# Left-over keys of P, left-overs of q and k, and whole q, turned as 64-row halves among P's halves

## The chip, the cores and the metric

The kernel runs on one core of a Trainium2 chip. The metric is the device time of one launch in microseconds, as the median of several runs; for each kernel one further execution is profiled. Engines are PE (TensorE, matmul, with PEld for its weight loads), DVE (VectorE), ACT (ScalarE), POOL (GpSimd) and SP (SyncE, which issues the DMAs here).

## The reference

Attention with a bias from the distance of positions, for 4 batches, 8 heads, 576 positions and 64 values per head, and then a layer x @ w_in, h * cos(h), @ w_out on the 2304 rows of its result.

```python
scores = scale * np.matmul(q, k.transpose(0, 1, 3, 2))      # q, k, v: 4 x 8 x 576 x 64
scores = scores + bias.transpose(2, 0, 1)[None, :, :, :]    # bias: a small MLP of log distances
attn = np.exp(scores - np.max(scores, axis=-1, keepdims=True))
attn = attn / (np.sum(attn, axis=-1, keepdims=True) + 1e-09)
x = np.matmul(attn, v)                                      # then as 2304 x 512
h = x @ w_in                                                # 512 x 2048
out = (h * np.cos(h)) @ w_out                               # 2048 x 512
```

All is float32.

## The kernel before

There are three stages: the bias table (to about 58 us), attention (to about 325 us) and the layer behind it. The change touches attention.

**Units and slots.** A unit is a pair of heads and one batch; there are 16, counted from 0. A unit has five jobs, in the order of query tiles 0, 1, 4, 2, 3. Tiles 0 to 3 hold 128 queries for each of the two heads; tile 4 holds the last 64 queries of both. The loop at the end of the attention code calls `slot(i)` for 80 jobs, five slots (j = 0 to 4) per unit, and five more calls stand among the first steps of the next stage. The order of work on each engine is the order of the program: nothing is moved by a scheduler, and each engine takes its instructions in turn.

**What a slot does**, in program order: `qk` makes the scores of this slot's job (L394, tile `s`), and DVE adds the bias and takes the extremum (L407). ACT takes the exponentials of the job before (L427). PE turns the normalised P of the job three slots back: `ptrans` flips it in halves of 64 rows (L456), row tile 0 and row tile 1 in turn, into the two PSUM tiles m0 and m1, eight pairs of flips for tiles 0 to 3 and five for tile 4. Where P has left-over keys 512 to 575 of both heads (tiles 0 to 3), `ptrans_left` turns them as one whole 128x128 block (L469) into the bank `t`, of which there is one. Then come the turns for the next unit (`turn`, L188): in slot 0 k, four whole blocks into bank `t`; in slot 1 "x", the 64 left-over rows of k and of q, one whole block beside the left-over of P in bank `t`; in slot 2 q, four whole blocks into `spare`, a buffer of the two that `s` has. Then PE multiplies earlier turned P with v (`pv`, L518). ACT copies m0 out of PSUM (`keep_main`, L476), then the turned k, x or q (`keep_turned`, L195 to L203), then, where a half of the unit is finished, the result (`keep_x`). DVE takes the row sums and their reciprocals (L439, L442), copies m1 and then the left-over (L479, tiles PT and PX). POOL splits k and q in two parts (L174, L178) and normalises P (L449). Between these, DVE, ACT and POOL widen weights for the next stage (L93 to L111); the weights' loads (L81, L86) are issued in slot 2 of odd units, behind DVE's last read of the buffer (L107).

**Loads.** All are issued by SP, in program order at the end of a slot, by `LOAD_PLAN`: q of the unit after the next in slot 0, k of three units on in slot 2 (two issues for rows 0 to 511 of the heads, L157, and two for the left-over rows of k and q, L160), v of the next unit in slot 4. Slot 1 of unit 0 also loads v of unit 0 and k of unit 2. Units 3, 7 and 11 load the bias of the next pair of heads (L218, L231), two or three issues a slot.

Of the kernel before, what the change touches and what calls it, by code (L numbers as in the profile page):

```python
# [9 lines left out]
F32 = mybir.dt.float32  # L10
# [3 lines left out]
AF = mybir.ActivationFunctionType  # L14
# [14 lines left out]
def kernel(  # L29
# [11 lines left out]
    nc = tc.nc  # L41
    B, H, S, D = q.shape
# [22 lines left out]
    ident = const.tile([128, 128], F32, name="ident")  # L65
# [47 lines left out]
    with tc.manual_schedule():  # L113
# [8 lines left out]
        ld = opened(front, "ld", 2, "right")  # L122
        lk = opened(front, "lk", 2, "right")
# [14 lines left out]

        nat = {}

        def load(u, x):
# [12 lines left out]
            m = 5 if x == "k" else 4  # L154
            t = (lk if x == "k" else ld).tile([128, m, 2, D], F32, tag=x, name=f"n{x}")
            for h in range(2):
                nc.sync.dma_start(out=t[:, 0:4, h], in_=pair_[h, 0:512].rearrange("(p r) d -> p r d", r=4))  # L157
            if x == "k":
# [4 lines left out]
            nat[u, x] = t  # L163

        def split(u, x, step=None):
            n = turned[x]
# [18 lines left out]
        def turn(u, x, ps):  # L185
            n = nat[u, "k" if x == "x" else x].rearrange("p r h d -> p r (h d)")
            for i, c in enumerate((4,) if x == "x" else range(4)):
                nc.tensor.transpose(ps[:, 128 * i : 128 * i + 128], n[:, c], ident)  # L188
            return ps

        def keep_turned(x, ps):
# [10 lines left out]
            o = turned[x][:, 64:576] if x == "k" else turned[x][:, 0:512]  # L202
            nc.scalar.activation(  # L203
                out=o.rearrange("p (x c) -> p x c", c=4),
                in_=ps.rearrange("p (c x) -> p x c", c=4),
                func=AF.Copy,
                scale=-0.125 if x == "q" else 1.0,
            )
# [46 lines left out]
        for x in "kq":  # L255
            load(0, x)
# [14 lines left out]
        pm = bank()  # L271
# [62 lines left out]
        tiles = [0, 1, 4, 2, 3]  # L334
# [35 lines left out]
        ps_s = opened(front, "ps_s", 2, "right", PSUM)  # L370
# [14 lines left out]
        def qk(u, j):  # L385
            t = tiles[j]
            heads = range(2 if t < 4 else 1)
            s = [ps_s.tile([128, 2, 512], F32, tag="s", name="s") for h in heads]
            for hf in range(2):
                for n, (a, b) in enumerate(((0, 0), (0, 1), (1, 0))):  # L390
                    for h in heads:
                        r = slice(64 * h, 64 * h + 64) if t < 4 else slice(0, 128)
                        o = HALF * hf + (64 if h == 0 else 0)
                        nc.tensor.matmul(  # L394
                            s[h][:, hf, 0:HALF],
                            qTs[u % 2][r, a, 128 * t : 128 * t + 128] if t < 4 else qTs[u % 2][:, a, 512:640],
                            kN[u][r, b, o : o + HALF],
                            start=(n == 0),
                            stop=(n == 2),
                            tile_position=(r.start, 0),  # L400
                        )
            hp = units[u][0]
            P[u, j] = pp.tile([128, 1152], F32, tag="p", name="P")
            for h in heads:
                neg = P[u, j][:, 576 * h : 576 * h + 576]
                m = sv.tile([128, 2], F32, tag=f"m{h}", name="m")
                nc.vector.tensor_tensor_reduce(  # L407
                    neg.rearrange("p (a x) -> p a x", a=2),
                    s[h][:, :, 0:HALF],
                    bias[hp, t, h].rearrange("p (a x) -> p a x", a=2),  # L410
                    1.0,
                    3.0e38,
                    ALU.add,
                    ALU.min,
                    m[:, 0:1],
                )
                cur[u, j, h] = (neg, m)
            if t == 4:
                return ps_s.tile([128, 2, 512], F32, tag="s", name="spare")[:, 0]

        P, dn, rc = {}, {}, {}

# [30 lines left out]

        def flip(out, i, r):
            p = slice(64 * r, 64 * r + 64)
            nc.tensor.transpose(out, i[p], ident[p, p], tile_position=(64 * r, 0))  # L456

        def ptrans(u, j):
            ps = [ps_m.tile([128, 512], F32, tag=f"m{r}", name="pm") for r in range(2)]
            cuts = [(256 * h + 64 * c, 640 * h + 128 * c) for h in heads_of((u, j)) for c in range(4)]  # L460
            if tiles[j] == 4:
                cuts.append((256, 512))
            for o, i in cuts:
                for r in range(2):
                    flip(ps[r][:, o : o + 64], P[u, j][:, i : i + 128], r)
            return ps

        def ptrans_left(u, j, ps):
            nc.tensor.transpose(ps, P[u, j][:, 512:640], ident)  # L469

        def where(j):
            t = tiles[j]
# [67 lines left out]
        ]  # L540
        T_EARLY = [(1, "k"), (1, "x"), (1, "q"), None, None]
        PV_EARLY = [[(-1, 0, (0, 1))], [(-1, 0, (2, 3))], [(-1, 0, (4,))], [(-1, 1, (0, 1, 2))], [(-1, 1, (3, 4))]]
        LOAD_PLAN = [[(2, "q")], [], [(3, "k")], [], [(1, "v")]]
        W_PLAN = [("abs", -1), (0, 0), (0.5, 2), (1, 5), (2, 7), ("load", 7), (3, 8), (4, 11)]
        get = lambda i: jobs[i] if 0 <= i < len(jobs) else None

        def slot(i):
            u, j = divmod(i, 5)
            now, last, prev = get(i), get(i - 1), get(i - 3)
            if now:  # L550
                spare = qk(u, j)
            if last:
                for h in heads_of(last):
                    softmax_exp(*last, h)
            if prev:
                if prev[1] in (0, 2):
                    alloc_half(prev[0], prev[1] // 2)
                pm = ptrans(*prev)
            left = prev and tiles[prev[1]] < 4
            tu, tx = T_EARLY[j] or (0, None)  # L560
            tx = tx if now and u + tu < NU else None
            t = bank() if left or tx in ("x", "k") else None
            if left:
                pl = t[:, 0:128]
                ptrans_left(*prev, pl)
            if tx:
                pt = turn(u + tu, tx, {"x": t and t[:, 128:256], "k": t, "q": spare}[tx])
            for du, hf, chunks in PV_EARLY[j]:
                if 0 <= u + du < NU:
                    pv(u + du, hf, chunks)  # L570
            if prev:
                keep_main(*prev, 0, pm[0])
            if tx:
                keep_turned(tx, pt)
            for du, hf, chunks in PV_EARLY[j]:
                if 0 <= u + du < NU and 4 in chunks:
# [17 lines left out]
            if now:  # L594
                if i == 1:
                    load(0, "v")
                    load(2, "k")
                for du, x in LOAD_PLAN[j]:
                    if u + du < NU:
                        load(u + du, x)  # L600
# [243 lines left out]
```

## Time and profile before

| | us |
|---|---|
| median of 3 runs | 727.86 (727.65 to 728.61) |
| the profiled execution | 730.44 |
| its span on the core | 728.60 |
| busy: PE, DVE, ACT, POOL | 712.5, 606.6, 443.9, 405.4 |

The span is the time from the first to the last instruction of the program in the profiled execution; the times of the rows count from its start. A row of a timeline has the start and the length of a run of equal instructions; matmuls are pipelined and their ends are modelled, so that one block's cost is read from its start to the start of the next.

### The profile page before, as it was taken

The numbers are of one execution on the slowest core, as the hardware profiler recorded it, in microseconds if no ns is written. First come the engines' busy times: TensorE is split into PE (matmuls) and PEld (weight loads), VectorE is DVE, ScalarE is ACT, GpSimd is POOL, SyncE is SP. The second block draws the span as 40 slices with busy tenths as digits, with TensorE's granted clock in tenths as the row PEclk, the third lists the DMA queues.
The fourth block names the chain that finished last, engine by engine and source line by source line (L and its number), as shares of the span: only waits on it lengthen the run. The fifth ranks groups of instructions, "written<-read, shape, count | busy, mean of one in ns | idle before, by whom it ended". The sixth has DMA issues, their size and how long they took to land.

```text
span 728.6 us, 15710 instructions
## 1 busy us (share of the span) xinstructions
PE 712.5 (98%) x5786; PEld 571.8 (78%) x5786; DVE 606.6 (83%) x1307; ACT 443.9 (61%) x947; POOL 405.4 (56%) x486
## 2 busy tenths in 40 slices
PE   6997999999999999999999999999999999999997
PEld 3575667766667667669989989988989989989986
DVE  8997788989889888856788789898999999966665
ACT  6897688787778878754565555445454454443342
POOL 0204678888877788874456373564554463663300
PEclk9999899999999999999999999999999999999999
DMA  6787328335432820201011010101011010011113
GB/s 202 239 303 210 91 66 229 78 82 141 135 94 64 232 47 18 76 1 30 30 50 38 32 57 29 59 30 58 30 35 53 29 59 30 0 43 45 45 43 88
DMA packets 84398, 58.65 MB, mean 80 GB/s; under 512 B 62304, under 2 KB 70624, under 8 KB 84320
## 3 DMA queue, kind: packets, MB, share of 16 engines
q1 hardware_dynamic: 84320, 57.63, 27.2%
q8 instruction: 46, 0.75, 0.4%
q14 instruction: 32, 0.26, 0.1%
HBM read 42.00 MB, written 15.61 MB: 79 GB/s over the span
## 4 chain that ended last, share of the span: by engine, by line
PE 95%; DVE 2%; POOL 1%; issue 1%; DMA 0%; ACT 0%; SPq 0%; DVEq 0%
PE ph L644 28%; PE po L699 28%; PE pv L518 13%; PE s L394 11%; PE pa L309 6%; PE pm L456 5%; PE pt L469 2%; PE pt L188 2%; DVE ht L293 1%; PE spare L188 1%; DMA lt<-in_ltab_dram 0%; POOL P L449 0%; DVE P L407 0%; DVE acc L722 0%; POOL kN L178 0%
## 5 line engine op out<-in xcount | busy, mean ns | idle before, releaser
L449 POOL TENSOR_SCALAR P<-P,rc 128x576 f32<-128x576 f32 x144 | 115.0, 812 | 75.7 <-ACT P L427 31.1
L407 DVE CUSTOM_DVE_ANT_0 P<-s,bt 128x576 f32<-128x576 f32 x144 | 103.8, 754 | 29.1 <-PE s L394 19.7
L648 ACT ACTIVATE a<-ph,quarter 128x384 int32<-128x384 f32 x96 | 55.8, 581 | 102.3 <-PE ph L644 101.0
L503 POOL TENSOR_TENSOR xs<-xT,xs 128x384 fp32r<-128x384 f32 x96 | 107.7, 1122 | 8.0
L427 ACT ACTIVATE P<-P,m 128x576 f32<-128x576 f32 x144 | 110.6, 771 | 2.1 <-DVE m L407 1.7
L644 PE MATMUL ph<-xs,wpre 128*128 128x384 f32 x576 | 109.4, 338 | 0.0
L654 DVE SCALAR_TENSOR_TENSOR r<-a,ph 128x384 f32<-128x384 int32 x96 | 52.8, 550 | 67.4 <-ACT a L648 67.2
L644 PE MATMUL ph<-xs,w 128*128 128x384 f32 x576 | 108.3, 337 | 0.0
L644 PEld LDWEIGHTS ph<-xs,wpre 128*128 128x128 f32 x576 | 101.8, 188 | 5.7 <-DVE a L663 0.9
L644 PEld LDWEIGHTS ph<-xs,w 128*128 128x128 f32 x576 | 101.5, 188 | 4.7 <-DVE a L663 0.6
L659 ACT ACTIVATE r<-r,hpi 128x384 f32<-128x384 f32 x96 | 59.3, 617 | 73.5 <-DVE r L655 73.3
L394 PEld LDWEIGHTS s<-kN,qT 64*128 64x128 f32 (+1 forms) x864 | 70.5, 188 | 40.8 <-issue 8.8
L394 PE MATMUL s<-kN,qT 64*128 64x288 f32 (+1 forms) x864 | 93.4, 315 | 4.0 <-DVE m L407 1.8
L502 POOL TENSOR_SCALAR xs<-xT 128x384 fp32r<-128x384 f32 x96 | 62.9, 656 | 39.9 <-PE ph L644 39.9
L518 PE MATMUL pv<-PT,vN 128*64 128x320 f32 (+1 forms) x512 | 76.9, 422 | 0.1
L673 DVE TENSOR_TENSOR gl<-a,gh 128x384 fp32r<-128x384 f32 x96 | 74.3, 774 | 2.2 <-ACT gh L667 2.2
L699 PE MATMUL po<-wpre,gh 128*128 128x512 f32 x288 | 75.3, 397 | 0.0
L699 PE MATMUL po<-w,gh 128*128 128x512 f32 x288 | 75.2, 395 | 0.0
L111 POOL TENSOR_TENSOR w<-wb,w 128x512 fp32r<-128x512 f32 x16 | 20.8, 1298 | 89.2 <-ACT w L109 89.2
L655 DVE SCALAR_TENSOR_TENSOR r<-a,r 128x384 f32<-128x384 int32 x96 | 60.6, 632 | 3.3
L667 ACT ACTIVATE gh<-a 128x384 fp32r<-128x384 f32 x96 | 49.8, 518 | 21.6 <-DVE a L663 21.6
L476 ACT ACTIVATE PT<-pm 128x512 f32<-128x512 f32 (+1 forms) x80 | 44.1, 551 | 30.8 <-PE pm L456 29.5
(83 smaller groups left out, 1220.1 us busy)
## 6 DMA issues: line engine op xcount, KB each, us to landing
sc<-rt SPq DMA_DIRECT2D x36, 295.5 KB, 3.3
raw<-in_moe_w_in_dram SPq DMA_DIRECT2D x16, 512.0 KB, 3.7
raw<-in_moe_w_out_dram SPq DMA_DIRECT2D x16, 512.0 KB, 3.6
bt<-sc SPq DMA_DIRECT2D x16, 288.0 KB, 4.0
nk<-in_k_dram SPq DMA_DIRECT2D x32, 128.0 KB, 3.1
nq<-in_q_dram SPq DMA_DIRECT2D x32, 128.0 KB, 2.9
bt<-sc SPq DMA_DIRECT2D x16, 256.0 KB, 4.0
vN<-in_v_dram SPq DMA_DIRECT2D x32, 128.0 KB, 2.6
```

The costliest lines, as they stand in the source:

```text
L394: nc.tensor.matmul(s[h][:, hf, 0:HALF], qTs[u % 2][r, a, 128 * t : 128 * t + 128] if t < 4 else qTs[u % 2][:, a, 512:640], kN[u][r, b, o : ...
L407: nc.vector.tensor_tensor_reduce(neg.rearrange("p (a x) -> p a x", a=2), s[h][:, :, 0:HALF], bias[hp, t, h].rearrange("p (a x) -> p a x", ...
L427: nc.scalar.activation(out=P[u, j][:, 576 * h : 576 * h + 576], in_=neg, func=AF.Exp, bias=m[:, 0:1], scale=-1.0, accum_out=dn[u, j][:, h ...
L449: nc.gpsimd.tensor_scalar(p, p, r, 1.0, ALU.mult, ALU.mult)
L502: nc.gpsimd.tensor_scalar(h, src, 1.0, 1.0, ALU.mult, ALU.mult)
L503: nc.gpsimd.tensor_tensor(l, src, f(h), ALU.subtract)
L518: nc.tensor.matmul(ps[64 * h : 64 * h + 64, 0 : WQ[hf]], a, m, start=(c == 0), stop=(c == 4), tile_position=(r.start, 64 * h), skip_group_ ...
L644: nc.tensor.matmul(ps, a, x, start=(i == 0), stop=(i == 3 * KD - 1))
L655: nc.vector.scalar_tensor_tensor(r, n, -TWO_PI_LO, r, ALU.mult, ALU.add)
L659: nc.scalar.activation(out=r, in_=r, func=AF.Sin, scale=SIN_SCALE, bias=hpi)
L673: nc.vector.tensor_tensor(gl, a, f(G[key][0]), ALU.subtract)
L699: nc.tensor.matmul(O[n][i], a[:, 128 * i : 128 * i + 128], w, start=(i0 == 0 and p == 0), stop=(i0 == GF - 1 and p == 2),)
```

## The change

P's left-over, x and q are no longer turned as whole blocks behind the flips. `halves` (in place of `ptrans` and `ptrans_left`) cuts each into two blocks of 64 rows, as P's own flips are, and puts them among P's flips: row tile 0 takes one flip of P, the left-over and x halves, the rest of P, then q; row tile 1 takes P, then q, then the left-over and x halves. The two halves of the left-over (and of x) go to the same bank `t`, so the last of row tile 0 and the first of row tile 1 are ordered through an empty instruction on SP (`follow`). q's halves go to the two banks of `spare`. q is then copied by ACT ahead of m0's copy. k in slot 0 is turned as before, and so are x and q in unit 0, which has no P yet. The load of k is cut in two: the two issues for the whole rows now stand in slot 1, the two for the left-over rows stay in slot 2.

```diff
+        def follow(first, then):
+            tc.add_manual_dep(
+                then.ins,
+                first.ins.name,
+                mybir.DependencyInfo(mybir.DependencyClass.Sync, mybir.DependencyReason.DATA),
+                reason="row tiles share a bank",
+            )
+            return then
+
+        def halves(u, j, left, x):
             ps = [ps_m.tile([128, 512], F32, tag=f"m{r}", name="pm") for r in range(2)]
             cuts = [(256 * h + 64 * c, 640 * h + 128 * c) for h in heads_of((u, j)) for c in range(4)]
             if tiles[j] == 4:
                 cuts.append((256, 512))
-            for o, i in cuts:
-                for r in range(2):
-                    flip(ps[r][:, o : o + 64], P[u, j][:, i : i + 128], r)
+            rows = []
+            for r in range(2):
+                at = slice(64 * r, 64 * r + 64)
+                main = [(ps[r][:, o : o + 64], P[u, j][:, i : i + 128]) for o, i in cuts]
+                one = [(left[:, at], P[u, j][:, 512:640])] if left is not None else []
+                one += [(o[:, at], i) for o, i in x.get("one", [])]
+                two = [(o[r], i) for o, i in x.get("two", [])]
+                rows.append(main[:1] + one + main[1:] + two if r == 0 else main + two + one)
+            made = [[flip(*pair_[r], r) for r in range(2)] for pair_ in zip(*rows)]
+            if one:
+                follow(follow(made[len(one)][0], nc.sync.nop()), made[-len(one)][1])
             return ps
-
-        def ptrans_left(u, j, ps):
-            nc.tensor.transpose(ps, P[u, j][:, 512:640], ident)
...
-        LOAD_PLAN = [[(2, "q")], [], [(3, "k")], [], [(1, "v")]]
+        LOAD_PLAN = [[(2, "q", None)], [(3, "k", 0)], [(3, "k", 1)], [], [(1, "v", None)]]
...
-                pm = ptrans(*prev)
+                pm = halves(*prev, pl, side_by_side(u + tu, tx, pt) if tx in ("x", "q") else {})
+            if tx and not (prev and tx in ("x", "q")):
+                turn(u + tu, tx, pt)
             for du, hf, chunks in PV_EARLY[j]:
                 if 0 <= u + du < NU:
                     pv(u + du, hf, chunks)
+            if tx == "q":
+                keep_turned(tx, pt)
             if prev:
                 keep_main(*prev, 0, pm[0])
-            if tx:
+            if tx and tx != "q":
                 keep_turned(tx, pt)
```

## Rows read from the trace of the kernel before

**Rows 1.** The page: busy time of each engine, and the chain by engine.

```profile
PE 712.5 (98%) x5786; PEld 571.8 (78%) x5786; DVE 606.6 (83%) x1307; ACT 443.9 (61%) x947; POOL 405.4 (56%) x486
...
PE 95%; DVE 2%; POOL 1%; issue 1%; DMA 0%; ACT 0%; SPq 0%; DVEq 0%
```

**Rows 2.** Windows: length, busy PE, PEld, DVE, ACT, POOL, clock, DMA share, GB/s.

```profile
122.30:130.05 7.75, 7.75 (x98) 5.98 (x99) 6.65 (x21) 7.64 (x22) 5.46 (x8) 1.00 0.76 200
```

**Rows 3.** Timeline of PE, unit 4: start, length, line, operation, operands, count.

```profile
123.05 0.47 PE L456 MATMUL pm<-ident,P 64*128 64x64 f32 x10
123.45 0.66 PE L188 MATMUL pt<-ident,nk 128*128 128x128 f32 x4
...
129.57 0.33 PE L469 MATMUL pt<-ident,P 128*128 128x128 f32 x1
129.74 0.60 PE L188 MATMUL spare<-ident,nq 128*128 128x128 f32 x4
130.27 0.65 PE L518 MATMUL pv<-PX,vN 64*64 64x256 f32 x4
...
131.97 0.77 PE L456 MATMUL pm<-ident,P 64*128 64x64 f32 x16
...
132.93 1.83 PE L518 MATMUL pv<-PT,vN 128*64 128x320 f32 x12
134.69 1.06 PE L394 MATMUL s<-kN,qT 64*128 64x288 f32 x12
135.60 0.66 PE L456 MATMUL pm<-ident,P 64*128 64x64 f32 x16
136.19 0.33 PE L469 MATMUL pt<-ident,P 128*128 128x128 f32 x1
136.45 0.76 PE L518 MATMUL pv<-PT,vN 128*64 128x320 f32 x4
```

**Rows 4.** Timelines of DVE and of POOL, unit 4, end of slot 2.

```profile
130.06 1.07 DVE L439 TENSOR_SCALAR dn<-dn 128x2 f32<-128x2 f32 x1 [0.16 <-ACT P L427]
...
131.25 0.67 DVE L479 COPY PT<-pm 128x512 f32<-128x512 f32 x1
131.84 0.28 DVE L479 COPY PX<-pt 128x128 f32<-128x128 f32 x1
...
129.84 1.27 POOL L111 TENSOR_TENSOR wpre<-wb,wpre 128x512 fp32r<-128x512 f32 x1
```

**Rows 5.** Timelines of DVE, SP and PE, unit 5, slots 2 and 3.

```profile
147.08 0.28 DVE L479 COPY PX<-pt 128x128 f32<-128x128 f32 x1
147.28 0.78 DVE L107 SCALAR_TENSOR_TENSOR wb<-raw,wb 128x512 uint32<-128x512 uint32 x1
...
148.12 0.37 SPq L81 DMA_DIRECT2D raw<-in_moe_w_in_dram  x1
...
148.71 1.57 PE L518 MATMUL pv<-PT,vN 128*64 128x320 f32 x10
```

**Rows 6.** Timelines of SP and PE at the start of attention.

```profile
72.82 0.62 SPq L160 DMA_DIRECT2D nk<-in_q_dram  x1
...
66.55 0.77 PE L456 MATMUL pm<-ident,P 64*128 64x64 f32 x16
...
73.66 0.73 PE L456 MATMUL pm<-ident,P 64*128 64x64 f32 x10
```

**Rows 7.** Windows (columns as in the second group) at the start of attention.

```profile
74.00:76.00 2.00, 2.00 (x16) 1.36 (x14) 1.96 (x7) 0.95 (x3) 0.08 (x1) 0.50 0.65 147
78.00:80.00 2.00, 2.00 (x30) 1.75 (x28) 0.77 (x3) 0.31 (x1) 0.65 (x1) 0.72 0.30 68
```

**Rows 8.** Groups by line and shape: busy us, mean ns, idle before.

```profile
L456 PE MATMUL pm<-ident,P 64*128 64x64 f32 x1184 | 54.0, 225 | 0.5 <-DVE PT L479 0.5
```

**Rows 9.** Timelines of SP and PE, unit 7, slot 1.

```profile
172.90 2.99 SPq L218 DMA_DIRECT2D bt<-sc  x6
...
173.04 0.66 PE L456 MATMUL pm<-ident,P 64*128 64x64 f32 x16
```

More of the change, by code (lines that the diff above doesn't have):

```diff
@@ L139, with load @@
         nat = {}
-        def load(u, x):
+        def load(u, x, part=None):
             hp, b = units[u]
@@ L154, in load @@
             m = 5 if x == "k" else 4
[L155 to L158, printed above, removed]
+            if part in (None, 0):
+                nat[u, x] = (lk if x == "k" else ld).tile([128, m, 2, D], F32, tag=x, name=f"n{x}")
+            t = nat[u, x]
+            if part in (None, 0):
+                for h in range(2):
+                    nc.sync.dma_start(out=t[:, 0:4, h], in_=pair_[h, 0:512].rearrange("(p r) d -> p r d", r=4))
+            if x == "k" and part in (None, 1):
                 for i, o in ((k, 0), (q, 64)):
@@ L162, in load @@
                     )
-            nat[u, x] = t
         def split(u, x, step=None):
@@ L189, in turn, with side_by_side @@
             return ps
+        def side_by_side(u, x, ps):
+            n = nat[u, "k" if x == "x" else x].rearrange("p r h d -> p r (h d)")
+            if x == "x":
+                return {"one": [(ps, n[:, 4])]}
+            return {"two": [([ps[:, r, 64 * c : 64 * c + 64] for r in range(2)], n[:, c]) for c in range(4)]}
         def keep_turned(x, ps):
@@ L202, in keep_turned @@
             o = turned[x][:, 64:576] if x == "k" else turned[x][:, 0:512]
+            if len(ps.shape) == 3:
+                nc.scalar.activation(
+                    out=o.rearrange("p (r x c) -> p r x c", r=2, c=4),
+                    in_=ps[:, :, 0:256].rearrange("p r (c x) -> p r x c", c=4),
+                    func=AF.Copy,
+                    scale=-0.125 if x == "q" else 1.0,
+                )
+                return
             nc.scalar.activation(
@@ L418, in qk @@
             if t == 4:
-                return ps_s.tile([128, 2, 512], F32, tag="s", name="spare")[:, 0]
+                return ps_s.tile([128, 2, 512], F32, tag="s", name="spare")
         P, dn, rc = {}, {}, {}
@@ L455, in flip @@
             p = slice(64 * r, 64 * r + 64)
-            nc.tensor.transpose(out, i[p], ident[p, p], tile_position=(64 * r, 0))
-        def ptrans(u, j):
+            return nc.tensor.transpose(out, i[p], ident[p, p], tile_position=(64 * r, 0))
+        def follow(first, then):
[4 more added lines that the diff above has]
+                reason="row tiles share a bank",
+            )
+            return then
+        def halves(u, j, left, x):
             ps = [ps_m.tile([128, 512], F32, tag=f"m{r}", name="pm") for r in range(2)]
@@ L554, in slot @@
                     softmax_exp(*last, h)
-            if prev:
-                if prev[1] in (0, 2):
-                    alloc_half(prev[0], prev[1] // 2)
-                pm = ptrans(*prev)
             left = prev and tiles[prev[1]] < 4
@@ L562, in slot @@
             t = bank() if left or tx in ("x", "k") else None
-            if left:
-                pl = t[:, 0:128]
-                ptrans_left(*prev, pl)
+            pl = t[:, 0:128] if left else None
             if tx:
-                pt = turn(u + tu, tx, {"x": t and t[:, 128:256], "k": t, "q": spare}[tx])
+                pt = {"x": t and t[:, 128:256], "k": t, "q": spare}[tx]
+                if tx == "q" and not prev:
+                    pt = spare[:, 0]
+            if prev:
+                if prev[1] in (0, 2):
+                    alloc_half(prev[0], prev[1] // 2)
+                pm = halves(*prev, pl, side_by_side(u + tu, tx, pt) if tx in ("x", "q") else {})
+            if tx and not (prev and tx in ("x", "q")):
+                turn(u + tu, tx, pt)
             for du, hf, chunks in PV_EARLY[j]:
@@ L597, in slot @@
                     load(2, "k")
-                for du, x in LOAD_PLAN[j]:
+                for du, x, part in LOAD_PLAN[j]:
                     if u + du < NU:
-                        load(u + du, x)
+                        load(u + du, x, part)
                 hp, b = units[u]
```

## The prediction

> **What bounds the kernel now.** I read the busy shares first, then the chain of work that ended last: PE is busy 98% of the span and carries 95% of the chain [rows 1]. So a TensorE instruction that goes away should be worth its time. The change acts only in the attention stage (units 0 to 15, about 58 to 325 us), so I then read that stage slot by slot in PE's timeline [rows 3], and there the picture is less simple. In unit 4, ACT has work for 7.64 of the 7.75 us from 122.30 to 130.05 [rows 2], from the first copy after slot 4 of the unit before to the last exponential of slot 2. DVE then takes up the row sums, and its copies out of PSUM end at 131.92 and 132.12 [rows 4]. PE's flips of slot 3 start at 131.97 [rows 3], 0.05 us after the first of these copies. PE is busy there, but it isn't alone in setting the pace. Last I read the queue of SyncE, because the change puts an instruction into it.
>
> **The prices of the turns.** A block costs its start to the next block's start [rows 3]. Five pairs of flips: 123.05 to 123.45, 0.40 us; eight pairs: 135.60 to 136.19, 0.59. So a pair costs 0.063 (0.19 over 3), and 0.08 comes on top for leaving the row tiles. Four whole turns of q take 0.53 (129.74 to 130.27). A left-over takes 0.17 where another whole turn follows (129.57 to 129.74) and 0.26 where pv follows (136.19 to 136.45). That makes 0.11 for a whole turn, 0.06 for coming in from row tiles, 0.095 for going on to pv.
>
> After the change a slot goes from flips straight to pv. That passage is not in the trace. Its bounds are 0 beyond the 0.08, and 0.15 (the 0.06 and 0.095 together, as if nothing were saved); I take 0.06, the row of the nearest kind, flips followed by another tiling.
>
> - A slot with a left-over alone: 0.59 + 0.26 = 0.85 becomes 9 x 0.063 + 0.08 + 0.06 = 0.71, a saving of 0.14. There are 36.
> - Slot 1, left-over and x: 0.59 + 0.17 + 0.20 = 0.96 becomes 10 x 0.063 + 0.14 = 0.77, saving 0.19, 14 times.
> - Slot 2, left-over and q: 0.59 + 0.17 + 0.53 = 1.29 becomes 13 x 0.063 + 0.14 = 0.96, saving 0.33, 14 times.
>
> For PE alone: 5.0 + 2.7 + 4.6 = 12.3 us (6.5 with 0.15 for the passage, 16.2 with 0). This is what the change could give at most.
>
> **What of it reaches the end.** In an even unit (unit 4 for the pattern) slot 3 cannot flip before the copies of slot 2 are done. They hang on ACT's unbroken work and on the row sums at 130.06, which took 1.07 us beside POOL's 1.27 us at 129.84 [rows 4]. None of this starts earlier when PE is faster, since it begins with ACT's copy at the end of slot 4's pv, after which ACT has no gap. There is a new tie as well: the left-over was turned after the eight pairs and now stands second, and it writes the one bank that the copy of slot 2's left-over must first empty (132.12). So slot 3 goes on at 132.17: eight pairs more, 0.51, and 0.14 give pv at 132.82 against 132.93. That is 0.11 instead of slots 1 to 3's 0.66; slot 4, where the copies are early, gives its 0.14. An even unit gains 0.25; seven of them (2 to 14) give 1.75 us. Moving q's copy ahead of the P copy on ACT costs nothing: that copy's bank is not wanted before slot 3's flips.
>
> The Trainium skill speaks against the change at this point: "TensorEngine Tiling (Array Packing)", Performance Considerations, PSUM Bottleneck, says that tiling speeds up TensorE but not the evacuation of PSUM, and that the copies may become the bound. The trace agrees by the 0.05 us between copy and flip. By the turns alone the time would be 715.6 us; by the rule it follows the copies.
>
> **The empty SyncE instruction.** It waits for the last left-over or x half of row tile 0, and the first one of row tile 1 waits for it. On PE all later turns and pv are queued behind that. Undisturbed, it has seven pairs of cover, 7 x 0.063 = 0.44 us (six in slot 1, eleven in slot 2). A flip takes 0.225 to its end [rows 8]; SyncE moved 0.06 after a release by DVE (148.06 to 148.12 [rows 5]); PE moved 0.05 after one (131.92 to 131.97). The sum is 0.34 and the instruction itself, so I cost it at 0. If its own time is that of the shortest issue shown, 0.37 [rows 5], it is 0.27 late; over the some 30 slots 3 and 4 without another delay that is up to 8 us.
>
> But SyncE runs in order, and it issues every load. Three places are not covered:
>
> - **The start.** Before unit 0's slot 3, SyncE has q, v and k loads of slots 0 to 2 queued, without a gap up to 73.44 (the last at 72.82, 0.62 us [rows 6]). PE starts that slot's flips at 66.55 and now stands at the ninth pair from about 67.1 to 73.55. The kernel before is at unit 1's first flips by 73.66 [rows 6]. The work still to be done up to there is the end of slot 3 (0.15), slot 4 (s, 134.69 to 135.60 in rows 3, 0.90, and 0.71 of flips) and the next s (0.90): 2.66 us at the full clock. The granted clock is 0.50 at 74 to 76 and 0.72 at 78 to 80 [rows 7], so half until about 79.1. Half the rate from 73.6 to 79.1 is 2.75 us of work, which just makes up that arrear, while the kernel before goes on by as much: at 79.1 the new one is some 2.7 us behind. Some 0.3 of it comes back, as the next slots then no longer wait for copies. I take a loss of 2.4; bounds 0 (the instruction is not behind the loads) and 3.5 (the clock comes back later).
> - **Weight loads** (slot 2 of odd units up to 11). The issue waits for DVE's step at L107, which ends at 148.06 in unit 5; the issue takes 0.37 and ends at 148.49 [rows 5], so PE goes on at about 148.6 and pv starts at 148.8, against 148.71. With slot 4's 0.14, units 5 and 9 give 0.1 together (unit 1 is in the start). Without the load, as in unit 13, the left-over goes at 147.41 (copy's end 147.36 [rows 5]) and pv at 148.05: 0.66 + 0.14 = 0.8.
> - **Bias loads** (units 3, 7, 11): six issues in 2.99 us from 172.90, of which three precede slot 1's instruction; the flips start at 173.04 [rows 9]. It runs at about 174.4 and is needed by 173.55, the ninth pair: PE stands 0.9 us. ACT and DVE, which set the pace of slot 3, go on meanwhile, so the unit is longer by 0 to 0.9, or by more where slot 3's issue is late as well. I take 0.4 a unit, a loss of 1.2 (bounds 0 and 3).
>
> The k load cut in two keeps two issues instead of four ahead of slot 3's instruction; the data is wanted a unit or more later, so it costs nothing itself.
>
> Unit 15 and the slots behind it have left-overs alone; I take 0.4 of their 1.0, as their slots 1 and 2 wait for copies too. The sum: 1.75 + 0.1 + 0.8 + 0.4 - 1.2 - 2.4 = -0.55 us of gain, a loss. The profiled execution took 730.44 us (span 728.6) and would take 731.0; on the median of 727.86, which lies 2.6 below that execution, it is 728.4.
>
> **The rivals.**
> - *The other engines follow.* If the ACT and DVE work of a unit moves forward with PE, most of 12.3 us less the 3.6 of SyncE's delays is left: between that and my sum, 719 to 725. For it: over the span ACT is busy 61% and DVE 83% [rows 1]. Against: the 0.05 us between rows 4 and 3, and ACT's 0.11 us of idle time [rows 2]. Chance 0.20.
> - *SyncE isn't behind its loads*, that is, the instruction runs where its two PE partners allow. Then 3.6 us less, 724.8, and odd units gain as unit 13 does: down to 721. Against: SyncE's issues in the trace are back to back in the program's order. Chance 0.10.
> - *The way through SyncE is longer than its cover* (the slower side). It decides from 0.44 us, that is 0.10 for the instruction itself; at 0.2 to 0.37 it costs 3 to 8 us: 731 to 736. For it: no row shows SyncE releasing PE. Against: all hops that are shown sum to 0.34. Chance 0.20.
> - *It doesn't do what it says*: halves of the left-over and of P don't overlap, since they go to different banks in turn. With 0.063 more for 134 pairs (64 of left-overs, 14 of x, 56 of q), 8.4 us come back to PE, of which the waits of rows 4 hide half: about 732.6. Chance 0.08.
>
> **How the numbers follow.** My own case has 0.42, with a range of its own from 726.5 to 731. The measurement tells about 0.2%, 1.5 us, from no change. Of the 0.42, 0.30 lies within it and 0.12 above. The first and second rivals are faster; of the third 0.18 is slower and 0.02 within; the fourth is slower. That gives faster 0.30, same 0.32, slower 0.38. The range 722 to 732.5 takes in the bounds of the start and of the bias loads and leaves out the far ends of the first and third rivals, about 0.2.
>
> **What will show it.** PE's blocks of flips should read 9, 10 and 13 pairs at 0.063, with pv next; if pairs cost 0.12 the fourth rival holds. In unit 0's slot 3 PE should stand still until SyncE's k issues end; if it does not, the second. In even units slot 3's second pair should start just after the copy of slot 2's left-over; if units are 0.7 us shorter, the first. In slot 4 a gap before the last pair would show the third. The forecast is wrong if the units' length falls by over 0.4 us, or rises at all in even units.

## The result: slower by 0.9%, and where the time went

The changed kernel takes 734.81 us (732.98 to 736.37), against 728.01 (727.65 to 728.61) for the kernel before on the same chip: a ratio of 1.0092, 95% interval 1.0071 to 1.0113. The forecast was 728.4, no change. Its profiled execution took 735.23 us, 4.8 more than the one of before (730.44).

The page of the changed kernel, its busy times and its chain by engine (as [rows 1]):

```profile
PE 703.4 (96%) x5920; PEld 569.6 (78%) x5920; DVE 604.8 (82%) x1307; ACT 443.4 (60%) x947; POOL 405.7 (55%) x486
...
PE 80%; DVE 7%; ACT 4%; POOL 3%; SPq 3%; issue 2%; DMA 1%; POOLq 0%; DVEq 0%; ACTq 0%
```

PE has 9.1 us less work and the kernel takes longer. PE's share of the chain falls from 95% to 80%, and SyncE's queue (SPq) holds 3% that it did not have. So the saving is real, and PE stands still elsewhere for more than it saved. The view of PE's waits says for whom (its first row: line waiting, line waited for, us in total, times, longest):

```profile
PE pt L472 <- SPq L498: 14.2, 11, 5.5
```

L472 is the flip, L498 the empty SyncE instruction. PE waits 14.2 us for it, in 11 of its 64 executions: 5.5 us in unit 0's slot 3, 1.3 in slot 3 of units 1, 5 and 9 (which load a weight), 4.4 in units 3, 7 and 11 (bias; slot 3, and once slot 2), and 3.0 in slot 1 of units 4, 8 and 12, behind the bias units. In before the view begins with `PE pa L309 <- DVE ht L293: 3.2, 8, 1.6`; there is no wait for SyncE in it.

**A slot without trouble.** PE's timeline of slots 2 to 4 in unit 4 (start, length, operation, count; as [rows 3]):

```profile
134.07 0.28 PE L472 MATMUL pm<-ident,P 64*128 64x64 f32 x2
...
134.62 0.47 PE L472 MATMUL spare<-ident,nq 64*128 64x64 f32 x8
134.87 0.22 PE L472 MATMUL pt<-ident,P 64*128 64x64 f32 x1
135.02 0.65 PE L548 MATMUL pv<-PX,vN 64*64 64x256 f32 x4
...
140.00 0.21 PE L472 MATMUL pm<-ident,P 64*128 64x64 f32 x2
...
140.49 0.22 PE L472 MATMUL pt<-ident,P 64*128 64x64 f32 x1
140.64 0.76 PE L548 MATMUL pv<-PT,vN 128*64 128x320 f32 x4
```

Thirteen pairs take 0.95 us (134.07 to 135.02) and nine take 0.64 (140.00 to 140.64). Here the tie costs nothing.

**Three slots with trouble.** First the start: SP and then PE, in unit 0's slot 3 (as [rows 6]; a bracket gives the idle time ahead and its releaser).

```profile
70.14 1.24 SPq L160 DMA_DIRECT2D nk<-in_k_dram  x2
71.42 0.63 SPq L163 DMA_DIRECT2D nk<-in_k_dram  x1
72.10 0.62 SPq L163 DMA_DIRECT2D nk<-in_q_dram  x1
...
66.64 0.66 PE L472 MATMUL pm<-ident,P 64*128 64x64 f32 x15
72.83 0.37 PE L472 MATMUL pt<-ident,P 64*128 64x64 f32 x1 [5.53 <-SPq L498]
```

SyncE is through with its last k issue at 72.72, and PE goes on at 72.83, after standing for 5.53 us.

Second a weight load, unit 5's slot 3 (as [rows 5]):

```profile
152.34 0.37 SPq L81 DMA_DIRECT2D raw<-in_moe_w_in_dram  x1
...
152.82 0.27 PE L472 MATMUL pt<-ident,P 64*128 64x64 f32 x1 [0.42 <-SPq L498]
```

Third a bias unit, unit 7's slot 3 (answers to [rows 9], which show its slot 1):

```profile
181.11 0.63 SPq L163 DMA_DIRECT2D nk<-in_k_dram  x1
181.80 0.62 SPq L163 DMA_DIRECT2D nk<-in_q_dram  x1
182.51 1.87 SPq L247 DMA_DIRECT2D bt<-sc  x2
184.48 0.52 SPq L86 DMA_DIRECT2D raw<-in_moe_w_out_dram  x1
...
182.88 0.68 PE L472 MATMUL pm<-ident,P 64*128 64x64 f32 x14
185.12 0.27 PE L472 MATMUL pt<-ident,P 64*128 64x64 f32 x1 [1.56 <-SPq L498]
```

Here k, bias and a weight queue one behind the other: the bias pieces end at 184.38, the weight's issue at 185.00, and PE, which was through with its flips at 183.56, stands for 1.56 us. The bias unit also troubles the next one: in unit 4's slot 1 the pieces from 127.75 hold q's load back to 130.43, and the tie stands behind it.

```profile
127.75 2.62 SPq L234 DMA_DIRECT2D bt<-sc  x3
130.43 1.26 SPq L160 DMA_DIRECT2D nq<-in_q_dram  x2
...
130.09 0.56 PE L472 MATMUL pm<-ident,P 64*128 64x64 f32 x12
131.80 0.27 PE L472 MATMUL pt<-ident,P 64*128 64x64 f32 x1 [1.15 <-SPq L498]
```

**Unit by unit.** A unit's length is taken from the first product of scores (`s`) of its slot 0 to that of the next unit:

| profiled execution, us | before | after | difference | forecast |
|---|---|---|---|---|
| start of unit 2 | 90.73 | 94.06 | +3.33 | +2.4 |
| units 2, 6, 10, 14 | 15.64 to 15.65 | 15.43 to 15.47 | -0.2 each | -0.25 each |
| units 3, 7, 11 | 15.77 to 15.78 | 16.53, 16.84, 16.85 | +0.75 to +1.08 | +0.4 each |
| units 4, 8, 12 | 15.67, 15.93, 15.68 | 15.95, 15.77, 15.77 | +0.28, -0.16, +0.09 | -0.25 each |
| units 5, 9 | 15.77, 15.78 | 15.70, 15.73 | -0.06 each | -0.05 each |
| unit 13 | 15.80 | 15.03 | -0.77 | -0.8 |

### The profile page after: what moved, and what is told of

The parts are those of the page before. It is cut to its first block, busy times and chain, and to the rows that moved or that the text cites. A ratio compares the mean times of both kernels' runs of the same rounds, so it can differ in the third digit from the quotient of the medians.

```text
span 733.4 us, 16080 instructions
## 1 busy us (share of the span) xinstructions
PE 703.4 (96%) x5920; PEld 569.6 (78%) x5920; DVE 604.8 (82%) x1307; ACT 443.4 (60%) x947; POOL 405.7 (55%) x486
## 3 DMA queue, kind: packets, MB, share of 16 engines
HBM read 42.00 MB, written 15.61 MB: 79 GB/s over the span
## 4 chain that ended last, share of the span: by engine, by line
PE 80%; DVE 7%; ACT 4%; POOL 3%; SPq 3%; issue 2%; DMA 1%; POOLq 0%; DVEq 0%; ACTq 0%
PE po L733 27%; PE ph L678 27%; PE pv L548 9%; PE s L410 6%; PE pa L325 6%; PE pm L472 3%; DVE P L423 2%; ACT P L443 2%; POOL P L465 2%; DVE dn L455 1%; PE pt L472 1%; DVE PT L509 1%; DVE ht L309 1%; SPq L160 1%; POOL qT L180 1%
## 5 line engine op out<-in xcount | busy, mean ns | idle before, releaser
L410 PE MATMUL s<-kN,qT 64*128 64x288 f32 (+1 forms) x864 | 90.9, 316 | 1.9 <-DVE m L423 1.6
L472 PE MATMUL pm<-ident,P 64*128 64x64 f32 x1184 | 64.5, 227 | 1.7 <-DVE PT L509 1.4
```

The costliest lines, as they stand in the source:

```text
L410: nc.tensor.matmul(s[h][:, hf, 0:HALF], qTs[u % 2][r, a, 128 * t : 128 * t + 128] if t < 4 else qTs[u % 2][:, a, 512:640], kN[u][r, b, o : ...
L472: return nc.tensor.transpose(out, i[p], ident[p, p], tile_position=(64 * r, 0))
```

## The experiments

All times are medians; "before" beside a kernel was run on the same chip. "Below the changed kernel" is against its median, 734.81, measured beside other runs of before (728.01); the ratio to before is the better measure. The diffs show the lines that matter. allfix, steadyfix, moved and leftlast were run ahead of konly, wonly, biasonly and wbias, so that the expectations of these four already know that all moves together help.

### What the turns bring, and what the tie costs

**notie.** The second half of the left-over and of x goes to a place of row tile 1's own bank that P's flips overwrite later, so that no bank is shared and no tie is needed; in row tile 1 these halves now stand ahead of P's flips, the copies take the first half twice, and the second halves are lost. The loads stay as in the changed kernel, with k cut in two.

```diff
+                if r:
+                    one = [(ps[1][:, 0:64], i) for o, i in one]
-                rows.append(main[:1] + one + main[1:] + two if r == 0 else main + two + one)
+                rows.append(main[:1] + one + main[1:] + two if r == 0 else one + main + two)
...
-            if one:
-                follow(follow(made[len(one)][0], nc.sync.nop()), made[-len(one)][1])
```

> The changed kernel without the SyncE instruction: the second half of the left-over and of x, row tile 1, goes to a place in bank m1 that P's flips write over (so these halves of the result are lost), and DVE and ACT copy the first half in their place. TensorE's work keeps its number and kind. Theory (the tie through SyncE is the loss, and ACT's and DVE's copies let only a part of the turns' saving through): units 2, 4, ... about 15.45 us, units 3, 5, ... 13 about 15.05 us, the start as before, in all about 721.5 us. Rival one (the halves themselves cost more than whole turns in this place): no faster than before, 727 or more. Rival two (nothing but TensorE sets the pace): every unit about 14.9, 716 us.

Measured: 721.61 us against 728.50, ratio 0.9900 (0.9884 to 0.9917). PE's timeline, first products of units 5, 6 and 7:

```profile
135.72 1.09 PE L410 MATMUL s<-kN,qT 64*128 64x288 f32 x12
...
150.69 1.08 PE L410 MATMUL s<-kN,qT 64*128 64x288 f32 x12
...
166.08 1.10 PE L410 MATMUL s<-kN,qT 64*128 64x288 f32 x12
```

Odd unit 14.97, even unit 15.39, against 15.77 and 15.65 before. The theory of the turns holds: 6.9 us are there to be had, and odd units give three times what even ones do. The load of k cut in two, which this kernel keeps, costs nothing to be seen.

**tieonly.** The kernel before with whole turns, plus the k load cut in two and a tie from its second flip of row tile 0 to its last of row tile 1.

```diff
...
+            made = [[flip(ps[r][:, o : o + 64], P[u, j][:, i : i + 128], r) for r in range(2)] for o, i in cuts]
+            if tiles[j] < 4:
+                follow(follow(made[1][0], nc.sync.nop()), made[-1][1])
```

> The kernel before, left-overs and q whole, with only the load of k cut in two and with the tie: the second flip of row tile 0, an empty SyncE instruction, the last flip of row tile 1, in every slot with a left-over. Theory (SyncE's queue is the loss): 3 to 3.5 us more in the first slots, about 1 us more in each of units 3, 7 and 11, and 0.2 to 0.3 in the odd units with a weight load: 734 to 735 us. Rival (the tie is covered, and the loss of the change comes from the order of the flips or the copies): 727.5 to 728.5 us.

Measured: 742.38 against 728.50, ratio 1.0194 (1.0171 to 1.0217). The direction is right and the size is not: +13.9. PE's waits:

```profile
PE pm L458 <- SPq L476: 10.8, 8, 5.2
```

Bias units 3, 7 and 11 are 18.09, 17.65 and 18.87 us long. Some 3 of the 13.9 us are not in this row. The granted clock is a place to look: it was 0.50 from 68.66 to 82.32, while in before it was back at 79.14 (shown further down), and again behind a stop of 1.18 us in unit 11, where before has the full clock:

```profile
68.66:82.32 13.66, 10.01 (x69) 7.58 (x71) 6.48 (x19) 5.26 (x14) 7.19 (x11) 0.50 0.38 85
253.00:256.40 3.40, 3.40 (x32) 2.76 (x32) 2.07 (x7) 1.67 (x5) 2.40 (x4) 0.50 0.80 216
```

Half the rate for 3.2 and for 3.4 us longer is, as an estimate, 3.3 us of work. The two halves of the change, measured apart, add up: -6.9 and +13.9 give +7.0, and the whole change measures +6.8. That they fit so well is partly luck: PE waits for the tie 10.8 us here and 14.2 in the changed kernel.

**qonly.** Only q in halves; left-over and x whole, loads as before, no tie.

```diff
-                pm = halves(*prev, pl, side_by_side(u + tu, tx, pt) if tx in ("x", "q") else {})
+                pm = halves(*prev, None, side_by_side(u + tu, tx, pt) if tx == "q" else {})
+            if left:
+                nc.tensor.transpose(pl, P[prev][:, 512:640], ident)
...
```

> Only q is turned in halves among P's flips, and copied by ACT first; left-over and x are whole turns behind the flips, loads are as before, and no bank is shared, so there is no SyncE instruction. TensorE alone: 14 times 0.28 us less, 724 us. Theory (DVE's copy of slot 2 holds slot 3's flips in even units): even units unchanged within 0.1, odd units 0.3 shorter, 725.5 to 726.5 us. Rival (the copies move forward with TensorE): all units 0.28 shorter, 724 us.

Measured: 724.98 (0.9950, 0.9935 to 0.9965), so 3.5 us of the gain, with no tie at all. Even units stay at 15.61 and odd ones fall to 15.29: as the theory says (the total lies between theory and rival), PE's saving in an even unit is eaten by the wait for slot 2's copies.

**leftlast.** notie, with row tile 0's halves behind P's flips instead of in front, second halves left out in the same way.

```diff
-                rows.append(main[:1] + one + main[1:] + two if r == 0 else one + main + two)
+                rows.append(main + two + one if r == 0 else one + main + two)
```

> The run without the tie, with the left-over and x halves of row tile 0 at the end of the flips instead of the second place (the second halves go again to a place that is written over, and are lost). Theory (in even units slot 3's second pair waits for the bank that DVE empties last): even units 0.1 to 0.2 shorter, odd ones the same: 720.5 to 721 us. Rival (the place does not matter, since P's own first flips wait nearly as long): 721.6 us, even units 15.40.

Measured: 721.46, against 721.61 for notie: no difference, as the rival said. Even units gain 0.05 (15.35), odd ones lose 0.05 (15.02). The early place of the left-over, which I had put down as a tie to the copy of slot 2, is not what limits an even unit.

### Moving what stands ahead of the tie

**startfix.** The changed kernel with its first loads spread over slots 1 to 8.

```diff
+        FIRST_LOADS = {1: [("k", 2, None)], 3: [("v", 0, None)], 4: [("q", 2, None), ("k", 3, 0)],
+                       5: [("k", 3, 1)], 8: [("v", 1, None)]}
...
-                if i == 1:
-                    load(0, "v")
-                    load(2, "k")
...
```

> The changed kernel with the loads of unit 0 moved: before the first tie only k of unit 2 is in SyncE's queue (four issues instead of twelve); v of unit 0 follows in slot 3, q of unit 2 and k of unit 3 in slots 4 and 5, v of unit 1 in slot 8. Theory (the stop in unit 0's slot 3, and the half clock that follows it, cost 3.3 us or more): 730.5 to 731.5 us, and the stretch at half clock is no longer than before, 6.8 us. Rival (the first slots are slow anyway by their data, and the loss is spread over the units): 734 to 735 us.

Measured: 730.81 against 728.50 (1.0026, 1.0011 to 1.0042), 4.0 below the changed kernel, as the theory said. PE's longest wait for SyncE falls from 5.5 to 1.4 us, and unit 2 begins at 88.23 in the profiled execution, the shortest of its ten (728.39).

**konly, wonly, biasonly, wbias.** One cause at a time. konly puts the k load whole into slot 3, behind that slot's tie; wonly the weight load behind the odd unit's last tie; biasonly spreads a pair's bias over two units; wbias makes the last two moves together.

```diff
-        LOAD_PLAN = [[(2, "q", None)], [(3, "k", 0)], [(3, "k", 1)], [], [(1, "v", None)]]
+        LOAD_PLAN = [[(2, "q", None)], [], [], [(3, "k", None)], [(1, "v", None)]]          # konly
-        W_PLAN = [("abs", -1), (0, 0), (0.5, 2), (1, 5), (2, 7), ("load", 7), (3, 8), (4, 11)]
+        W_PLAN = [("abs", -1), (0, 0), (0.5, 2), (1, 5), (2, 7), (3, 8), ("load", 9), (4, 11)]   # wonly
+        BIAS_PLAN = {(0, 0): 4, (0, 1): 0, (0, 2): 1, (1, 1): 2, (1, 2): 3}                 # biasonly
...
```

> The changed kernel with one move: the k load stands whole in slot 3, after that slot's tie, as against half in slot 1 and half in slot 2. Theory (the tie is late wherever SyncE issues loads ahead of it; in the trace of the changed kernel the empty instruction of unit 0's slot 3 ran at 72.77, right behind the four issues of a k half from 70.14 to 72.72, and TensorE stood 5.53 us; with k elsewhere it ran at 69.97 and TensorE stood 0.81): the start gains 3.5 to 4.3, even units 15.62 to 15.42 (7 x 0.2), bias and weight units unchanged: 729 to 730.5. Rival (the start's stop is made good later, since the other engines run behind at the start anyway): under 1.5 us of gain, 733 to 734.

Measured: 731.68 (1.0064, 1.0044 to 1.0083), 3.1 below the changed kernel and between theory and rival; the interval overlaps that of the changed kernel (1.0071 to 1.0113), so that the size of the gain is uncertain. In the profiled execution, the shortest of its four (729.42), unit 2 begins at 88.68 in place of 94.06. The part on the even units was wrong: units 2, 6, 10 and 14 stay at 15.44 to 15.53, and the mean of all even units only falls from 15.61 to 15.59.

> The changed kernel with one move: the load of a weight stands at the odd unit's slot 4, behind the last tie of the unit, as against ahead of it. Theory: slot 3 of units 1, 5, 9 (4.28 to 4.30 in the changed kernel, 3.62 in unit 13, which loads no weight) becomes 3.62, and units 3, 7, 11 gain as much: 6 x 0.65 = 3.9 us, 730.5 to 731.5. Rival (in the bias units SyncE stands for the bias chain anyway, so only units 1, 5, 9 gain): 2 us, 732.5 to 733.

Measured: 734.86 (1.0095, 1.0076 to 1.0113), no gain at all; both expectations were wrong on the total. Units 5 and 9 did fall, to 15.02, and units 3, 7 and 11 by 0.5 to 0.95. But units 4, 8 and 12 rose to 17.78, 16.46 and 15.94: their tie in slot 1 is now still later. Unit 4's in PE's timeline:

```profile
131.37 0.27 PE L472 MATMUL pt<-ident,P 64*128 64x64 f32 x1 [1.72 <-SPq L498]
```

and the granted clock soon behind it (window, length, busy PE, PEld, DVE, ACT, POOL, clock, DMA share, GB/s):

```profile
132.84:136.25 3.41, 3.41 (x34) 2.88 (x35) 2.06 (x8) 1.95 (x5) 2.43 (x3) 0.50 0.71 157
```

> The changed kernel with one move: the five pieces of a pair's bias are spread over two units (slots 0, 1, 2 of the odd one, 1 and 2 of the even one), as against all in the odd one. Theory: units 3, 7, 11 fall from 16.38, 16.68, 16.68 to the 15.55 to 15.70 of units 5 and 9, and units 4, 8, 12 from 15.96, 15.94, 15.77 to 15.62: about 3.4 us, 731 to 732. Rival (the bias chain waits on SyncE wherever it stands and takes its price to another slot): under 1.5 us, 733.5 to 735.

Measured: 735.06 (1.0094, 1.0075 to 1.0113), no gain, just above the time that the rival named. Units 3, 7 and 11 stay at 16.78 to 16.88: their slot 3 still has a weight load ahead of its tie, behind the bias and the k half.

> The changed kernel with the two moves that gave nothing alone: the weight load behind the odd unit's last tie, and the bias spread over two units; the k load and the first loads as in the changed kernel. Theory (the issues share one queue: with either move alone the other's issues still stand ahead of a tie, so only both clear it): units 3, 7, 11 at 15.05 to 15.2, units 4, 8, 12 at 15.4 to 15.7, start as in the changed kernel, 7 us less than it: 727 to 728.5. Rival (the bias chain costs what it costs wherever it stands, and the gain of the kernel with all moves came by the k load): 732 to 734.5.

Measured: 731.92 (1.0041, 1.0028 to 1.0054), 2.9 below the changed kernel, just under the rival's range and far from the theory's. Units 5, 9 and 13 run at 15.01 to 15.03, but units 3, 7 and 11 at 16.73, 16.52 and 16.21. SP and PE in unit 3 show what is left:

```profile
116.25 0.63 SPq L163 DMA_DIRECT2D nk<-in_k_dram  x1
116.93 0.62 SPq L163 DMA_DIRECT2D nk<-in_q_dram  x1
117.65 2.44 SPq L234 DMA_DIRECT2D bt<-sc  x3
...
118.06 0.68 PE L472 MATMUL pm<-ident,P 64*128 64x64 f32 x14
120.20 0.27 PE L472 MATMUL pt<-ident,P 64*128 64x64 f32 x1 [1.47 <-SPq L498]
```

Half of the k load and three pieces of bias are queued from 116.25 to 120.09, ahead of the tie; PE stood for it from 118.73.

**steadyfix.** All three moves together. "The run above" in its expectation is allfix, which comes next here.

> As the run above, but the first loads of unit 0 stay in slots 0 to 1, so that the first tie stands behind ten issues. Theory: the units are 8.3 us shorter in all than in the changed kernel (from the difference of its units to those without the tie), the start 1 us: 725 to 726.5 us, and the difference of this run to the one above, 4 us, is the start. Rival (the start's stop is made good by the units that follow): the same time as the run above within 1 us.

Measured: 723.68 (723.39 to 724.61) against 728.27, ratio 0.9931 (0.9914 to 0.9948): 11.1 below the changed kernel and 4.6 faster than before, with no part of the work left out, and below its own theory. The same view of unit 3 as above:

```profile
112.45 2.12 SPq L234 DMA_DIRECT2D bt<-sc  x3
115.11 1.26 SPq L160 DMA_DIRECT2D nk<-in_k_dram  x2
...
114.70 0.68 PE L472 MATMUL pm<-ident,P 64*128 64x64 f32 x14
115.19 0.22 PE L472 MATMUL pt<-ident,P 64*128 64x64 f32 x1
115.34 1.83 PE L548 MATMUL pv<-PT,vN 128*64 128x320 f32 x12
```

The bias ends at 114.57, the tie passes, and the k load follows at 115.11; PE never stops. Unit 3 is 15.01 us long, as without a tie. The moves do not add: 3.1 alone and 2.9 for the other two make 6.0, together they give 11.1. A tie is late as long as one of the three is ahead of it.

**allfix.** The same with the first loads spread as well.

```diff
+        FIRST_LOADS = {1: [("k", 2, None)], 3: [("v", 0, None)], 4: [("q", 2, None), ("k", 3, None)],
+                       7: [("v", 1, None)]}
```

> The changed kernel, whole, with SyncE's issues moved out of the way of the tie: k in slot 3, the weight load in slot 4, the bias of the next heads in slots 0 to 2 of the last unit and 1 and 2 of the unit behind it, and the first loads spread as before slot 3 only k of unit 2 is left. Theory (all of the loss is the tie waiting behind issues, none its own way): the time of the run without the tie, 721.6, and up to 1 us more: 721.5 to 722.5 us; units 15.4 (even) and 14.95 (odd). Rival (the way through SyncE costs some 0.1 us a slot by itself): 725 to 730 us.

Measured: 724.07 (721.96 to 724.78), ratio 0.9927 (0.9912 to 0.9942): between theory and rival, and no better than steadyfix, as steadyfix's rival said. I had costed the start at 4 us here by startfix, but steadyfix had already taken most of it by moving k: PE's waits for SyncE sum to 0.8 us in steadyfix and 0.7 here. In the profiled pair unit 2 still begins 1.85 earlier (87.73 against 89.58), and the medians don't show it. The trace of allfix is of the shortest of its six executions (721.96), and its granted clock was 0.50 for 6.8 us in the first slots (63.66 to 70.50), that of steadyfix for twice as long:

```profile
63.06:76.72 13.66, 12.60 (x96) 10.80 (x96) 9.28 (x32) 8.05 (x22) 9.49 (x13) 0.50 0.68 168
```

Half the rate for 6.8 us longer costs up to 3.4 us of work, so the 1.85 need not be a gain of the moved loads. Both medians lie 2.1 to 2.5 above notie's 721.61, and only 0.7 to 0.8 of that is waiting for SyncE; the rest stays open.

**moved.** The kernel before, no halves and no tie, with the load moves of allfix.

> Control: the kernel before, left-overs, x and q whole and no tie, with the moved loads of the first of these runs. Theory (loads were never late before, so moving them gives nothing): 728 to 729 us. Rival (the earlier or later loads, those of the first slots above all, are what made the run without the late issues faster): 725 us or less.

Measured: 728.06 against 728.27, ratio 0.9998 (0.9987 to 1.0009). The moves are worth nothing without the tie.

**The sum of it.** For each profiled execution its own time, the wait of PE for the empty instruction, and the length of the stretches at half clock (0.50, read from windows of 1 us between 55 and 330 us):

| kernel | profiled execution | PE waits for SyncE, times | less the wait | half clock |
|---|---|---|---|---|
| after | 735.23 | 14.2, 11 | 721.0 | 13.6 |
| biasonly | 732.69 | 11.2, 8 | 721.5 | 6.8 |
| wonly | 733.92 | 12.6, 8 | 721.3 | 13.6 |
| wbias | 732.08 | 8.3, 7 | 723.8 | 17.1 |
| konly | 729.42 | 7.8, 13 | 721.6 | 10.2 |
| startfix | 728.39 | 7.5, 10 | 720.9 | 0 |
| allfix | 721.96 | 0.7, 3 | 721.3 | 6.8 |
| steadyfix | 723.60 | 0.8, 1 | 722.8 | 13.7 |
| notie | 722.39 | none | 722.4 | 10.2 |

The times spread over 13 us, and without the wait over 2.9. notie takes the tie away, steadyfix takes the issues away from in front of it, and either removes the whole loss; moved shows that the moves give nothing by themselves. That shows the cause of the loss: PE stands behind SyncE's queue. What is left, up to 3 us, is not explained by the waits. The highest remainder, wbias, has the longest stretch at half clock and the lowest, startfix, has none, but the rest do not fall in line: a part of it may be the clock, which is not shown.

## Why the prediction was wrong

That the tie would wait behind SyncE's loads was right; where in the bias units and behind them it would stop PE was not, and the waits were priced too low. The miss is 6.4 us (734.81 against 728.4), of which 4.2 lie in the sum (735.23 in place of 731.0 for the profiled execution) and 2.2 in the step from there to the median. The steps that failed in the sum, largest first: the bias units (priced at slot 1, 1.2 us, where slot 3 made them 2.9), the units behind them (put down for the gain of an even unit, where they lost), the start (2.4 in place of 3.3) and the end (a gain of 0.4 that did not come).

- **The prices of the turns: right.** Thirteen pairs take 0.95 (forecast 0.96), nine 0.64 (0.71, since the passage to pv costs nothing where I took 0.06). Ten pairs with x take 0.71 in unit 5's slot 1 (145.83 to 146.54), where I had 0.77; in unit 7's slot 1 it is 0.89, as the tie came behind bias pieces that were issued until 177.66 and PE went on at 177.78. Halves of P and of the left-over do overlap, which rules out the fourth rival.
- **Even units: right.** The forecast was a gain of 0.25; it was 0.2 in the changed kernel and 0.26 without the tie (15.65 to 15.39). The reason holds too. In unit 6's slot 3 DVE and PE read (as [rows 4]):

```profile
166.82 0.67 DVE L509 COPY PT<-pm 128x512 f32<-128x512 f32 x1
167.41 0.28 DVE L509 COPY PX<-pt 128x128 f32<-128x128 f32 x1
...
167.55 0.27 PE L472 MATMUL pm<-ident,P 64*128 64x64 f32 x1 [0.23 <-DVE PT L509]
167.84 0.25 PE L472 MATMUL pt<-ident,P 64*128 64x64 f32 x1
```

PE waits for the first copy (167.49) and, with the left-over, goes on after the second (167.69); leftlast shows that the second costs an even unit only 0.05. Without the tie an odd unit got all of the 0.80 that its turns save, an even unit 0.26: of 12.3 us of PE's saving 6.9 arrived. The rule that the prediction cited from the Trainium skill, "TensorEngine Tiling (Array Packing)", Performance Considerations, PSUM Bottleneck, held in the even units; the page says that the copy may become the bound after a 4x speedup, and here there are two row tiles.
- **Undisturbed, the tie costs nothing: right.** The empty instruction takes 17 ns (below), and slot 4's tie never stops PE in the slots shown. Odd units are 15.01 to 15.03 long in steadyfix and 14.95 to 14.99 in notie; the order of the flips, which differs too, may be the whole of that, as leftlast has 15.02 without a tie. The third rival named 731 to 736 us and the time fell there, but its mechanism, a long way through SyncE in every slot, is not what the trace shows. The second did not hold either, since PE stood until the k issues ended, nor the first, since even units did not become 0.7 shorter.
- **The start: mis-sized, 3.33 in place of 2.4.** PE stood where it was forecast, and went on at 72.83 (forecast 73.55). The step that failed is "half until about 79.1". I had taken the end of the half clock from the kernel before, and in the changed one's profiled execution it came later. The stretch at half clock in the kernel before:

```profile
72.31:79.14 6.83, 6.61 (x48) 4.99 (x50) 3.12 (x9) 2.59 (x7) 4.34 (x6) 0.50 0.57 129
```

and in the changed kernel:

```profile
68.13:81.78 13.65, 8.94 (x67) 6.90 (x69) 6.74 (x23) 5.97 (x16) 7.54 (x10) 0.50 0.41 92
```

  Half the rate for 2.64 us longer is 1.3 us of work, of which 0.9 shows in the start of unit 2. But the stop does not fix that end. biasonly has the same program up to unit 2, and its PE stood 5.17 us and went on at 72.83 too; its half clock was over at 76.14, and its unit 2 began at 91.82, 1.1 later than before's 90.73:

```profile
69.32:76.14 6.82, 3.31 (x32) 2.97 (x32) 1.72 (x7) 0.99 (x3) 3.35 (x5) 0.50 0.38 85
...
91.82 1.07 PE L410 MATMUL s<-kN,qT 64*128 64x288 f32 x12
```

  So 3.33 holds for one execution, and the clock's return was no fixed point to add up from. Three of the changed kernel's four executions had the mean granted clock of the profiled one, 0.989.
- **Bias units: mis-sized, 2.9 in place of 1.2.** The forecast priced slot 1 alone (0.9 late, 0.4 arriving). The tie of slot 1 hardly stopped PE; it is slot 3's that does (1.25, 1.56 and 0.94 us in units 3, 7 and 11, and 0.65 in unit 11's slot 2), as the pieces of slots 1 and 2, the k halves and the weight load all queue ahead of it. "Or by more where slot 3's issue is late as well" is in the text, but it was put into the bound (3), and it was the case.
- **Units 4, 8 and 12: not foreseen, 1.0 us.** Put down for a gain of 0.75 together, they lost 0.2, as PE stood 1.15, 0.87 and 0.96 us in their slot 1. I gave them the pattern of unit 4, in a kernel where no tie asks when SyncE is done with the bias. SyncE's arrears from the bias unit reach their slot 1.
- **Weight loads: right** (-0.06 and -0.77, forecast -0.05 and -0.8). wonly shows that moving them gives units 5 and 9 the same 0.7.
- **Unit 15 and behind: 0.5 too much.** I took a gain of 0.4; the rest of the span moved by less than 0.1.
- **From the profiled execution to the median: 2.2 us.** The profiled execution of before lies 2.4 above its median, and I took 2.6 off the sum for that. The changed kernel's lies 0.4 above its own. A surplus that belongs to one execution was carried over as if it belonged to the kernel.

The range ended at 732.5. It had room for the bounds of the start and of the bias units (3.5 and 3) even added up: 728.4 and 1.1 and 1.8 are 731.3. What carried the time out of it are terms without any bound: the units behind the bias units (1.0), the end (0.5) and the offset of one execution (2.2).

## What to carry to other kernels

An engine that runs in order is no place for an ordering instruction unless everything queued ahead of it, in every kind of loop pass, ends before the partner needs it: write out the queue slot by slot, the rare slots (bias, weights, the start) above all, for they made nearly all of the loss here. When such a tie is needed, move the loads behind it in the program's order; here the moves were worth 11.1 us together, 6.0 when summed one set at a time, and nothing without the tie. No run put the tie on an engine that issues no loads, or gave each half of the left-over a bank of its own to be copied from. A row of one execution with a disturbance of its own is no offset for the next kernel's median.

## What the runs showed of the hardware

The empty SyncE instruction takes 17 ns in all 64 executions (its line in the changed kernel: shortest, median and longest ns):

```profile
L498 SPq EVENT_SEMAPHORE  x64: 17/17/17, 72.8 to 324.0; - x64
```

An issue of one of the attention's or the weights' DMAs on the same queue takes 0.34 (L86) to 0.64 us (L247) at the median of its line in the changed kernel, some 20 to 40 times as much. So a hop through SyncE costs little, and a place in its queue costs much.

A stop of PE can cost more than its own length when the clock falls behind it. In wonly PE stood 1.72 us up to 131.37, and from 132.84 to 136.25 the granted clock was 0.50, the 1.2 GHz level. In the changed kernel the half clock began at 68.13, soon after PE stopped, and lasted to 81.78, 9 us after it went on. But the first slots of attention fell to half clock without a stop for the tie too: notie, which has no tie, stood at 0.50 for 10.2 us, and steadyfix from 63.06, 6 us before its tie first stopped PE:

```profile
68.76:79.00 10.24, 9.97 (x73) 7.70 (x75) 6.74 (x20) 5.88 (x16) 8.15 (x11) 0.50 0.49 110
```

In startfix, whose longest wait for SyncE was 1.4 us, the profiled execution had the full clock from 60 to 88 us:

```profile
60.00:88.00 28.00, 23.65 (x279) 17.20 (x277) 22.43 (x69) 21.39 (x56) 20.50 (x27) 1.00 0.59 152
```

Not each stop had that effect: behind the 1.56 us of unit 7 the clock stayed up. What decides it no run here tells.
